# Cutting the last loads of a one-token decode kernel differently: a quarter block by a DMA of 124 rows and one of four

## The chip, the cores and the metric

The kernel runs on one core of one Trainium2 chip. The metric is the device time of one execution in microseconds, as the median of several runs. Lower is better.

## The reference

One token `x` of 1024 elements goes through two branches, and a scalar gate mixes their results (shapes are float32; the cut keeps what is computed).

```python
g = sigmoid((x * gate_w).sum(-1))
# branch A: attention over a cache; 32 query heads, 4 key/value heads, 65536 positions, head size 128
q = x @ wq                                   # 1024 -> 32 heads x 128
scores = einsum("bhqd,bhkd->bhqk", q, k) * 128 ** -0.5     # k, v: (1, 4, 65536, 128), each shared by 8 heads
a = einsum("bhqk,bhkd->bhqd", softmax(scores), v).reshape(1, 1, 4096) @ wo
# branch B: a gated feed-forward layer on the one token, scaled by its router weight
r = x @ w_r
y = (silu(x @ w_gate) * (x @ w_up)) @ w_down # 1024 -> 3584 -> 1024
b = x + y * sigmoid(r)
out = g * a + (1 - g) * b
```

Nearly all bytes are the two caches, 134 MB each; with the projections and the feed-forward weights some 346 MB are read once.

## The kernel before

**Streaming.** Everything large comes from HBM through three buffers of 128 partitions x 16384 floats (`stream`, called `st` in the profile). SyncE (SP) issues all these loads from one queue, in the order of one loop (lines 119 to 133). The first 36 loads (`heads`) are wq, the caches and wo of the four key/value groups, 8 MB each. Then come six tiles of `ffn`, 14336 floats per row: two of w_gate, two of w_up and two of w_down. A load waits on SP until TensorE has marked the buffer's last use (`marked`, line 124).

**Blocks of w_down.** w_down is cut into 28 blocks of 128 rows; a block is 1024 floats in each partition (`D` = 1024). Tile 4 holds blocks 0 to 13, tile 5 blocks 14 to 27. These two tiles come by several DMAs, each with a semaphore of its own (`end0`, `end1`, ...), cut at the columns in `ENDS` (line 34). Before, tile 5 comes by six DMAs: blocks 14 to 19, 20 to 23, 24 and 25, 26, the first 768 columns of block 27, and its last 256. In TensorE's program the helper `tail` (lines 364 to 374) waits for a DMA's semaphore when the first column asked of it is that DMA's first column.

**The last products.** TensorE (PE) takes blocks 0 to 23 in matmuls of 512 columns into the PSUM tile `att`, which already holds the attention's result folded over 128 partitions (the loop that ends with `mark(ins, "early")`). VectorE (DVE) then adds `att` to `att_sb`, which holds the gated attention and the residual (`dve.tensor_add` at line 277): this is the early sum. The last four blocks (24 to 27; `EARLY` = 24) go to two other PSUM tiles, `y` for the first 192 columns of each quarter of the output and `acc` for the last 64 (`PIECES`), by four matmuls of 32 output partitions per tile and block; the profile counts each of them twice, so that a block is 8 on `y` and 8 on `acc`. The early sum is brought into the same tiles by eight products with the small matrix `halves` (line 404). Before, these stand with block 26, each ahead of the product of that block with the same output partitions, and TensorE waits for the early sum (`take("d2p")`, line 399) ahead of block 26.

**The end.** ScalarE (ACT) copies `y`, VectorE copies `acc`, and SP writes the 4 KB result with one DMA of four rows and waits for it (lines 134 to 140).

**Small loads.** ScalarE issues two small loads at the start: `xk` of 128 rows and `x_row` of two rows.

Of the kernel before, what the change touches and what calls it, by code (L numbers as in the profile page):

```python
# [8 lines left out]
P = 128  # L9
D = 1024  # L10
G = 4
# [9 lines left out]
NQ = D // 4  # L21
# [6 lines left out]
PER = UNITS // 2  # L28
BUFS = 3

TAIL = 14336
NTAIL = 3 * KB * F // TAIL

ENDS = {NTAIL - 2: [8 * D, TAIL], NTAIL - 1: [6 * D, 10 * D, 12 * D, 13 * D, 13 * D + 768, TAIL]}

PIECES = [(0, 192), (192, NQ)]

EARLY = 24
# [13 lines left out]
def gated_mix_kernel(nc, x, vecs, heads, ffn, out):  # L52
# [21 lines left out]
    pe, act, dve, pool, sp = nc.tensor, nc.scalar, nc.vector, nc.gpsimd, nc.sync  # L74

    stream = [nc.alloc_sbuf_tensor(f"st{b}", [P, 2 * CH], F32, align_bytes=256)[:, :] for b in range(BUFS)]
# [35 lines left out]
    names = ["done", "fed", "x0", "x1", "x2", "acted", "pooled", "marked", "d2p", "d2a", "d2s", "self"]  # L112
    names += [f"ld{b}" for b in range(BUFS)] + [f"end{i}" for i in range(sum(map(len, ENDS.values())))]
    sems = {n: nc.alloc_semaphore(n) for n in names}
# [4 lines left out]
    ends = []  # L119
    for i in range(G * PER + NTAIL):  # L120
        b = i % BUFS
        if i >= BUFS:
            g, l = divmod(i - BUFS, PER)
            sp.wait_ge(sems["marked"], MARK[f"{LAST[l]} {g}" if g < G else ["gate 0", "gate 1", "up 0"][l]])
        if i < G * PER:
            sp.dma_start(stream[b], heads[i]).then_inc(sems[f"ld{b}"], 16)
        elif i - G * PER not in ENDS:
            sp.dma_start(stream[b][:, :TAIL], ffn[i - G * PER]).then_inc(sems[f"ld{b}"], 16)
        else:
            cuts = ENDS[i - G * PER]  # L130
            for c0, c1 in zip([0] + cuts, cuts):
                sp.dma_start(stream[b][:, c0:c1], ffn[i - G * PER, :, c0:c1]).then_inc(sems[f"end{len(ends)}"], 16)  # L132
                ends.append((i, c0, c1))
    sp.wait_ge(sems["acted"], ACTED["first"])
    sp.wait_ge(sems["d2s"], 1)
# [45 lines left out]
    c0, c1 = PIECES[0]  # L181
# [97 lines left out]
    c0, c1 = PIECES[1]  # L279
# [5 lines left out]
    def mark(ins, name):  # L285
        marks.append(name)
        ins.then_inc(sems["marked"])

    def take(name, n=1):
        pe.wait_ge(sems[name], n).then_inc(sems[name], -n)  # L290
# [73 lines left out]
    def tail(first, n):  # L364
        i, c = divmod(first, TAIL)
        assert c + n <= TAIL
        if i < min(ENDS):
            if c == 0:
                take(f"ld{(G * PER + i) % BUFS}", 16)
        else:  # L370
            for e, (i1, c0, _) in enumerate(ends):
                if (i1 - G * PER, c0) == (i, c):
                    pe.wait_ge(sems[f"end{e}"], 16)
        return stream[(G * PER + i) % BUFS][:, c : c + n]


    for i, part in enumerate(("gate", "up")):
        ps = (ps_f, ps_u)[i]
        for k in range(KB):
            for e in range(2):  # L380
                for j in range(4):
                    ins = pe.matmul(  # L382
                        ps[32 * j : 32 * j + 32, e, :FN], xp[:, k, :], tail((i * KB + k) * F + (2 * j + e) * FN, FN),
                        start=(k == 0), stop=(k == KB - 1),
                    )
            if k % 4 == 3:
                mark(ins, f"{part} {k // 4}")
    take("d2p")
    for b in range(EARLY):
        for f in range(2):  # L390
            j = 2 * (b % 2) + f
            ins = pe.matmul(  # L392
                att[32 * j : 32 * j + 32, :], hp[:, 32 * b : 32 * b + 32], tail(2 * KB * F + b * D + f * 512, 512),
                start=(b < 2), stop=(b >= EARLY - 2),
            )
    mark(ins, "early")
    for b in range(EARLY, FB):
        if b == EARLY + 2:
            take("d2p")
        for bank, (c0, c1) in zip(banks, PIECES):  # L400
            n = c1 - c0
            for j in range(4):
                if b == EARLY + 2:
                    pe.matmul(  # L404
                        bank[32 * j : 32 * j + 32, :n], halves[:, j // 2, :],
                        att_sb[:, j % 2 * NQ + c0 : j % 2 * NQ + c1], start=False, stop=False,
                    )
                at = 4 * c0 + j * n if b == FB - 1 else j * NQ + c0
                ins = pe.matmul(  # L409
                    bank[32 * j : 32 * j + 32, :n], hp[:, 32 * b : 32 * b + 32], tail(2 * KB * F + b * D + at, n),  # L410
                    start=(b == EARLY), stop=(b == FB - 1),
                )
            if b == FB - 1:
                mark(ins, "first" if c0 == 0 else "last")
# [32 lines left out]
```

## Time and profile before

| | us |
|---|---|
| median of 3 runs | 805.84 (805.73 to 806.34) |
| the profiled execution | 805.78 |
| its span, first to last instruction | 804.5 |

| engine | busy us | share of the span |
|---|---|---|
| PE (matmul) | 407.5 | 51% |
| DVE | 72.3 | 9% |
| ACT | 44.8 | 6% |

The span leaves out what lies around the program's instructions: 805.78 - 804.5 = 1.28 us. PE is TensorE's matmul row, PEld its weight loads, SPq an instruction that SP's queue issues (a DMA here). In a timeline row stand the start and the duration in us, the engine, the line, the operation, the tiles written and read, the shape, the count, and in brackets how long the engine sat idle before it and what ended that. In a row of stretches the last three columns are the granted clock of TensorE, the mean busy share of the 16 DMA engines and the rate in GB/s; a packet counts in the stretch in which it starts, so that a share can pass 1.

### The profile page before, as it was taken

Reading aid. Unit: us, or ns where it says so; the run is one execution under the profiler, and the core shown is the slowest. Engines: PE = TensorE matmul, PEld = TensorE weight load, DVE = VectorE, ACT = ScalarE, POOL = GpSimd, SP = SyncE. Lnnn points to the kernel's source line nnn. Section 1 sums busy time; section 2 is a strip of 40 time slices with the busy share of each in tenths; the row PEclk is TensorE's granted clock in tenths of the full one; section 3 lists DMA queues with packets and bytes.
Section 4 is the critical chain, followed back from the end, with each engine's and each line's share of the span. In section 5 each row is a group of like instructions: output and inputs, shape, how many; then the busy total and the mean of one; then the engine's idle time right before and its main releaser. Section 6 shows DMA issues by size and latency. Waiting matters only on the chain. (4 is left out here: it accounts for less than half of the span.)

```text
span 804.5 us, 6124 instructions
## 1 busy us (share of the span) xinstructions
PE 407.5 (51%) x2826; PEld 122.0 (15%) x2826; DVE 72.3 (9%) x135; ACT 44.8 (6%) x100; POOL 2.5 (0%) x13
## 2 busy tenths in 40 slices
PE   0544464455654564545544454456444545464466
PEld 0211111111111121111111111112111111121122
DVE  0200010000000020000100110000000100000310
ACT  0000030000000030000000110000000300000000
POOL 1000000000000000000000000000000000000000
PEclk9977767768767677677877586777776866787778
DMA  9999999999999999999999999999999999999998
GB/s 418 417 418 466 415 424 460 417 428 453 420 430 450 424 431 446 427 430 446 427 430 443 430 430 443 430 431 430 440 433 427 443 430 430 429 448 426 439 413 342
DMA packets 7078, 346.20 MB, mean 430 GB/s; under 512 B 918, under 2 KB 1050, under 8 KB 1308
## 3 DMA queue, kind: packets, MB, share of 16 engines
q1 hardware_dynamic: 6920, 346.04, 99.4%
q8 instruction: 8, 0.13, 0.1%
q10 hardware_dynamic: 148, 0.02, 0.0%
q14 instruction: 2, 0.02, 0.0%
HBM read 346.05 MB, written 0.00 MB: 430 GB/s over the span
## 5 line engine op out<-in xcount | busy, mean ns | idle before, releaser
L326 PE MATMUL ps_u<-st,qp 128*32 128x512 f32 x1024 | 152.5, 759 | 149.1 <-PEq L290 149.1
L338 PE MATMUL acc<-st,pt 128*32 128x512 f32 x1024 | 152.3, 757 | 144.1 <-PEq L290 144.1
L338 PEld LDWEIGHTS acc<-st,pt 128*32 128x32 f32 x1024 | 43.5, 135 | 250.0 <-issue 250.0
L326 PEld LDWEIGHTS ps_u<-st,qp 128*32 128x32 f32 x1024 | 41.4, 135 | 256.3 <-issue 256.3
L171 ACT ACTIVATE s<-ps_u 128x512 f32<-128x512 f32 x32 | 19.1, 597 | 560.4 <-PE ps_u L326 560.4
L240 DVE TENSOR_REDUCE mx<-s 128x1 f32<-128x512 f32 x32 | 22.0, 686 | 284.2 <-ACT s L171 284.2
L255 DVE STREAM_TRANSPOSE pt<-s 128x512 f32<-128x512 f32 x32 | 22.7, 711 | 198.0 <-PE acc L338 194.4
L310 PE MATMUL ps_u<-st,xp 128*32 128x512 f32 x128 | 23.3, 893 | 22.1 <-PEq L290 22.1
L382 PE MATMUL ps_u<-st,xp 128*32 128x448 f32 x128 | 17.1, 703 | 16.9 <-PEq L290 16.9
L382 PE MATMUL ps_f<-st,xp 128*32 128x448 f32 x128 | 16.8, 691 | 13.3 <-PEq L290 13.3
L176 ACT ACTIVATE s<-s,nb 128x512 f32<-128x512 f32 x32 | 22.6, 708 | 10.4 <-DVE nb L250 10.4
L392 PE MATMUL att<-st,s 128*32 128x512 f32 x96 | 14.9, 776 | 7.5 <-DMA st<-in_ffn 4.9
L355 PE MATMUL att<-st,op 128*32 128x512 f32 x128 | 14.6, 594 | 2.4 <-PEq L290 2.4
L301 PE MATMUL ps_m<-dsum,ones 128*128 128x2 f32 x2 | 0.6, 350 | 23.5 <-PEq L290 23.5
L310 PEld LDWEIGHTS ps_u<-st,xp 128*32 128x32 f32 x128 | 5.9, 158 | 40.1 <-issue 40.1
L382 PEld LDWEIGHTS ps_u<-st,xp 128*32 128x32 f32 x128 | 5.3, 139 | 28.6 <-issue 28.6
L259 DVE COPY s<-acc 128x512 f32<-128x512 f32 x4 | 2.8, 692 | 71.6 <-PE acc L338 71.6
L382 PEld LDWEIGHTS ps_f<-st,xp 128*32 128x32 f32 x128 | 5.2, 135 | 25.1 <-issue 25.1
L229 DVE COPY s<-ps_u 128x512 f32<-128x512 f32 x4 | 2.8, 692 | 53.5 <-PE ps_u L310 53.5
L179 ACT ACTIVATE s<-ps_f 128x896 f32<-128x896 f32 x1 | 0.9, 917 | 105.4 <-PE ps_f L382 105.4
L392 PEld LDWEIGHTS att<-st,s 128*32 128x32 f32 x96 | 3.7, 134 | 18.6 <-issue 10.7
L332 PE MATMUL ps_m<-md,ones 128*128 128x128 f32 x8 | 1.8, 311 | 8.2 <-PEq L290 8.2
(69 smaller groups left out, 68.9 us busy)
## 6 DMA issues: line engine op xcount, KB each, us to landing
st<-in_ffn SPq DMA_DIRECT2D x4, 7168.0 KB, 43.3
st<-in_ffn SPq DMA_DIRECT2D x2, 3072.0 KB, 37.1
st<-in_ffn SPq DMA_DIRECT2D x1, 4096.0 KB, 34.9
st<-in_ffn SPq DMA_DIRECT2D x1, 2048.0 KB, 36.9
st<-in_ffn SPq DMA_DIRECT2D x1, 1024.0 KB, 38.9
st<-in_heads SPq DMA_DIRECT2D x36, 48.1
st<-in_ffn SPq DMA_DIRECT2D x1, 512.0 KB, 39.7
st<-in_ffn SPq DMA_DIRECT2D x1, 384.0 KB, 40.2
```

What stands on the lines that cost most here:

```text
L171: tell(act.activation(scores[:, c, :], ps_s[c % 2], AF.Copy), f"s{c} {g}")
L176: act.activation(t, t, AF.Exp, bias=nb, scale=SCALE, accum_out=sums[:, c : c + 1]), f"e{c} {g}"
L229: to_pe(dve.tensor_copy(q_sb, ps_s[0]))
L240: ins = dve.tensor_reduce(mx[:, c : c + 1], scores[:, c, :], AX.X, ALU.max)
L255: to_pe(dve.transpose(pts[:, c % 2, :], scores[:, c, :]))
L259: to_pe(dve.tensor_copy(o_sb, acc.rearrange("p (s d) -> p s d", s=4)))
L310: ins = pe.matmul(ps_s[0][32 * j : 32 * j + 32, :], xp[:, k, :], unit(0)[:, k * D + f * 512 : k * D + (f + 1) * 512], start=(k < 2), stop= ...
L326: ins = pe.matmul(ps_s[c % 2][32 * j : 32 * j + 32, :], qp[:, 32 * s : 32 * s + 32], unit(1 + c)[:, (4 * s + j) * 512 : (4 * s + j + 1) * ...
L338: ins = pe.matmul(acc[32 * j : 32 * j + 32, :], pts[:, c % 2, 32 * m : 32 * m + 32], unit(1 + NCH + c)[:, m * 512 : (m + 1) * 512], start= ...
L355: ins = pe.matmul(att[32 * j : 32 * j + 32, :], op[:, h, :], unit(UNITS - 1)[:, h * D + f * 512 : h * D + (f + 1) * 512], start=False, sto ...
L382: ins = pe.matmul(ps[32 * j : 32 * j + 32, e, :FN], xp[:, k, :], tail((i * KB + k) * F + (2 * j + e) * FN, FN), start=(k == 0), stop=(k == ...
L392: ins = pe.matmul(att[32 * j : 32 * j + 32, :], hp[:, 32 * b : 32 * b + 32], tail(2 * KB * F + b * D + f * 512, 512), start=(b < 2), stop= ...
```

## The change

Tile 5 of the feed-forward weights is cut at other columns, so that it comes by eight DMAs in place of six. Block 24 comes in two parts. Its first 768 columns are one DMA of 128 rows. Its last 256 columns (`NARROW`) are two DMAs on one semaphore: partitions 0 to 123, then partitions 124 to 127 (`ROWS`); TensorE waits for 32 on that semaphore. Blocks 25 and 26 come by one DMA. The two parts of block 27 stay as they were. The eight products of the early sum, and the wait for it, move from block 26 to block 25.

```diff
-ENDS = {NTAIL - 2: [8 * D, TAIL], NTAIL - 1: [6 * D, 10 * D, 12 * D, 13 * D, 13 * D + 768, TAIL]}
+ENDS = {NTAIL - 2: [8 * D, TAIL], NTAIL - 1: [6 * D, 10 * D, 11 * D - NQ, 11 * D, 13 * D, 13 * D + 768, TAIL]}
+
+NARROW, ROWS = (NTAIL - 1, 11 * D - NQ), [(0, 124), (124, P)]
...
             for c0, c1 in zip([0] + cuts, cuts):
-                sp.dma_start(stream[b][:, c0:c1], ffn[i - G * PER, :, c0:c1]).then_inc(sems[f"end{len(ends)}"], 16)
+                for r0, r1 in ROWS if (i - G * PER, c0) == NARROW else [(0, P)]:
+                    sp.dma_start(
+                        stream[b][r0:r1, c0:c1], ffn[i - G * PER, r0:r1, c0:c1]
+                    ).then_inc(sems[f"end{len(ends)}"], 16)
                 ends.append((i, c0, c1))
...
                 if (i1 - G * PER, c0) == (i, c):
-                    pe.wait_ge(sems[f"end{e}"], 16)
+                    pe.wait_ge(sems[f"end{e}"], 16 * len(ROWS) if (i, c) == NARROW else 16)
...
     for b in range(EARLY, FB):
-        if b == EARLY + 2:
+        if b == EARLY + 1:
             take("d2p")
         for bank, (c0, c1) in zip(banks, PIECES):
             n = c1 - c0
             for j in range(4):
-                if b == EARLY + 2:
+                if b == EARLY + 1:
                     pe.matmul(
                         bank[32 * j : 32 * j + 32, :n], halves[:, j // 2, :],
                         att_sb[:, j % 2 * NQ + c0 : j % 2 * NQ + c1], start=False, stop=False,
                     )
```

## The prediction

> **What bounds the kernel now.** I read the page first, its queues and its chain of waits.
>
> ```profile
> span 804.5 us, 6124 instructions
> DMA  9999999999999999999999999999999999999998
> q1 hardware_dynamic: 6920, 346.04, 99.4%
> q8 instruction: 8, 0.13, 0.1%
> q10 hardware_dynamic: 148, 0.02, 0.0%
> ```
>
> The DMA engines are busy in all 40 slices, and only the last slice falls under nine tenths. The change leaves the bytes as they are, so all that it can move lies in the last few microseconds. The chain of waits, asked for its last stretch, and the timeline of that stretch show what they hold.
>
> ```profile
> 759.67 0.33 SPq L132
> ...
> 760.52 38.89 DMA st<-in_ffn
> ...
> 801.73 0.11 PE acc L409 x6
> 801.84 0.37 PE y L409 x8
> ```
>
> ```profile
> 792.17 6.77 PE L392 MATMUL att<-st,s 128*32 128x512 f32 x40 [4.46 <-DMA st<-in_ffn]
> 797.02 0.16 PEld L392 LDWEIGHTS att<-st,s 128*32 128x32 f32 x8 [1.23 <-DMA st<-in_ffn]
> ...
> 799.01 0.69 DVE L277 TENSOR_TENSOR s<-att,s 128x512 f32<-128x512 f32 x1 [20.00 <-PE att L392]
> 799.45 0.16 PEld L409 LDWEIGHTS y<-st,s 128*32 128x32 f32 x8 [1.42 <-DMA st<-in_ffn]
> 799.46 0.53 PE L409 MATMUL y<-st,s 128*32 128x192 f32 x8 [0.51 <-DMA st<-in_ffn]
> ...
> 799.92 0.51 PE L409 MATMUL y<-st,s 128*32 128x192 f32 x8
> ...
> 800.35 0.49 PE L404 MATMUL y<-s,halves 128*32 128x192 f32 x2
> 800.72 0.11 PEld L409 LDWEIGHTS y<-st,s 128*32 128x32 f32 x1 [0.26 <-DMA st<-in_ffn]
> ...
> 801.67 0.53 PE L409 MATMUL y<-st,s 128*32 128x192 f32 x8
> ...
> 802.02 0.29 PE L409 MATMUL acc<-st,s 128*32 128x64 f32 x8
> 802.27 0.33 ACT L182 ACTIVATE s<-y 128x192 f32<-128x192 f32 x1 [58.66 <-PE y L409]
> ```
>
> TensorE waits for loads at 797.02 (blocks 20 to 23), at 799.45 (24 and 25) and at 800.72 (26). From there it has no gap: the eight early-sum products and block 26 fill 800.72 to 801.67, and block 27 follows at once, by the chain behind TensorE's own work (801.73, 801.84). The loads end at the same moment, as the stretches of the end show (the last three columns are TensorE's clock, the DMA share and GB/s):
>
> ```profile
> 799.90:800.10 0.20, 0.20 (x20) 0.17 (x15) 0.00 (x0) 0.00 (x0) 0.00 (x0) 1.00 0.82 312
> 800.10:800.30 0.20, 0.20 (x13) 0.17 (x9) 0.00 (x0) 0.00 (x0) 0.00 (x0) 1.00 0.66 256
> 800.30:800.50 0.20, 0.20 (x13) 0.17 (x6) 0.00 (x0) 0.00 (x0) 0.00 (x0) 1.00 0.57 225
> ...
> 800.70:800.90 0.20, 0.20 (x5) 0.17 (x8) 0.00 (x0) 0.00 (x0) 0.00 (x0) 1.00 0.52 210
> 800.90:801.10 0.20, 0.20 (x11) 0.17 (x7) 0.00 (x0) 0.00 (x0) 0.00 (x0) 1.00 0.39 154
> 801.10:801.30 0.20, 0.20 (x15) 0.20 (x7) 0.00 (x0) 0.00 (x0) 0.00 (x0) 1.00 0.45 159
> ...
> 801.60:801.80 0.20, 0.20 (x17) 0.20 (x13) 0.00 (x0) 0.00 (x0) 0.00 (x0) 1.00 0.00 0
> ```
>
> The sixteen DMA engines don't end together. Times 16, the shares say that six or seven are done by about 800.3, two or three more (the middle ones) by about 800.9, and six or seven, the late ones, run to about 801.6. So there are early engines 1.2 to 1.6 us ahead of the last, middle ones some 0.7 to 1.2 ahead, and late ones. Every load is complete only when the last engine has delivered. TensorE's clock is at full grant there.
>
> **How many engines the new loads use.** The queues' packets tell how a load is spread. q1 carries 48 loads of 128 rows (36 of heads, four whole tiles, two and six parts) and the four-row result: 48 x (128 + 16) + 4 + 4 = 6920. q10 carries 128 rows and two rows: 128 + 16 + 2 + 2 = 148. So beside its rows a load leaves 16 small packets for 128 rows, four for four rows and two for two, one per engine at work, and each engine gets the same number of rows. A number of at most 16 that divides 124 into equal shares is 1, 2 or 4; the trace has no such load, and the ends are one engine and, with unequal shares, sixteen. I take four, since the two-row and four-row loads took the largest number that divides them. The Trainium skill, "DMA: Bandwidth & Descriptors", section "Why a DMA increments its semaphore by 16 and not by 1", states that rule, the largest number up to 16 that divides both sides' outer size, and that from SP it is the lowest-numbered engines; the packet counts agree with the first half, and no view here numbers engines.
>
> Then 128 rows of 1 KB fall on four engines, 32 each, where block 24's part of a whole load put eight on each of sixteen.
>
> **Part 1, the loads.** Per engine the stretches between TensorE's wake-ups give the prices: 799.45 - 797.02 = 2.43 us for 64 KB (eight rows of 8 KB), 800.72 - 799.45 = 1.27 for 32 KB, 801.67 - 800.72 = 0.95 for 24 KB (rows of 3 KB), and at most 802.02 - 801.67 = 0.35 for eight rows of 1 KB, since TensorE was at work there too. A row of 1 KB thus costs between 2430 / 64 = 38 and 350 / 8 = 44 ns, and 32 of them 1.2 to 1.4; I take 1.3.
>
> On the twelve other engines, the late ones among them, what follows 797.02 is now 0.95 (block 24's first part), 2.43 (25 and 26), 0.95, 0.35: 0.32 us less than before. Blocks 25 and 26 are there at 797.02 + 0.95 + 2.43 = 800.40. On the four it is 1.3 more, less what they are ahead:
> - early engine (1.4 ahead): 800.30, before the others, so it costs nothing
> - middle engine (0.95 ahead): 797.02 - 0.95 + 0.95 + 1.3 + 2.43 = 800.75
> - late engine: 801.70
>
> The issue costs nothing:
>
> ```profile
> L132 SPq DMA_DIRECT2D st<-in_ffn x8: 328/432/858, 742.7 to 761.9; - x8
> DMA to landing us min/median/max: 32.5/39.3/41.8
> ```
>
> Two more issues are two times 0.43 us on SP, and block 27's loads go out 0.9 us later; what hides it are the 32.5 us or more that a load stands in the queue. Without that cover the end would move by those 0.9. Behind them on SP stands only the wait for the result.
>
> **Part 2, TensorE.** A block without the early sum takes 799.92 - 799.46 = 0.46 us, the one with it 0.95 from its data (its first pair of products with `halves`, at 800.35, ran ahead of the wait). Before, 24 and 25 were done while 26 was under way, and 0.95 followed the last load but two. Now blocks 25 and 26 arrive together, so 0.95 + 0.46 = 1.41 us follow their landing, ahead of block 27. With 0.32 us saved on the load and 0.46 added behind it, block 27 starts at 800.40 + 1.41 = 801.81 even where the four engines delay nothing: 0.14 later than 801.67. With a middle engine among the four it starts at 800.75 + 1.41 = 802.16, 0.49 later; with a late one at 801.70 + 1.41 = 803.11, 1.44 later. Block 27's own loads are no bound in these cases: on the middle engine they land at 801.70 and 802.05, and their products start at 802.16 and 802.51. From there on the end is as before.
>
> The wait for the early sum now stands one block earlier, with all of TensorE's remaining work behind it. TensorE ends block 23 at 792.17 + 6.77 = 798.94, does block 24 until about 799.4, and waits until VectorE is done at 799.01 + 0.69 = 799.70. That is 0.7 us before 800.40, so block 25's load hides it; without that cover it would cost 0.3. The narrow load is wanted in block 24, at about 799.1, and on a middle engine it lands at 797.02 - 0.95 + 0.95 + 1.3 = 798.3.
>
> **Sum.** The forecast is the middle engine: +0.49. The profiled execution took 805.78, its span plus 1.28, and the median is 805.84, 0.06 more and inside the runs' spread; 805.84 + 0.49 = 806.3. About 0.2%, or 1.6 us, is what a measurement of this kernel can tell from no change, so this would count as none.
>
> **The rivals.**
>
> *A late engine among the four*: block 27 starts 1.2 to 1.44 later (the late ones lie within 0.2), 807.0 to 807.3. For it: six or seven of sixteen are late, so four drawn blindly would nearly always hold one. Against it: q8 has eight loads of some 16 KB, and following packets through the trace by end and start (no view groups them by engine), the seven late engines are those that carried one each, while the two engines of the two-row load are one early and one middle. If small loads always take the same first engines, and q8 goes from one engine to its neighbour, the other two of the four are clear of it in most places that its run can have.
>
> *Only early engines in the four, or packets and PE overlap better*: +0.14 down to a gain of 0.32, if TensorE's 1.41 could shrink to the 0.95 between block 26's load and the next: 805.5 to 806.0. Against it, the rows from 800.72 to 801.67 have no gap to take out, and one of the two known engines is middle.
>
> *Not confined*: the 124 rows go to sixteen engines, eight each. Then every engine has 0.35 more than without the narrow load, and blocks 25 and 26 land at 800.40 + 0.35 = 800.75: also 806.3, by another way.
>
> *A fixed hold, slower*: each of the two small loads keeps its engine for the round trip of a load that stands alone, instead of streaming with its neighbours. The nearest row is SP's wait for the 4 KB result:
>
> ```profile
> SPq L140 <- DMA out<-s: 1.1, 1, 1.1
> ```
>
> Two holds of 1.1 on the middle engine give 800.75 + 2.2 = 802.95 and block 27 at 804.36: +2.7, 808.5. It decides the sign from a hold of (1.6 - 0.49) / 2 = 0.56 each. Against it: block 27's two loads followed each other within 0.35. The same page of the skill, section "Anatomy of one DMA", gives a fixed cost of about 2 us per DMA; by that the two would cost up to 4 us on these engines, and the trace's back-to-back small loads contradict it inside a full queue. Fewer than four engines (two of 62 and two rows: 64 x 0.041 = 2.6 in place of 1.3) would end near there too, at +1.8, 807.6.
>
> **Chances.** Middle engine 0.47, not confined 0.06, only early engines or a small gain 0.12, a late engine 0.17: all of these lie within 0.2%, 0.82 together, of which I give 0.03 to a late engine with packets dearer than 44 ns, over 1.6 us, so 0.79 remain. Fixed hold or fewer engines 0.14, which with those 0.03 makes slower 0.17. Faster by over 1.6 us 0.04: nothing in the rows gives it, since the engines' whole unevenness is 1.6. The range leaves out most of the gains and the fixed hold: from 805.6, a little under the early case, to 807.4, a late engine with dear packets. The likeliest case alone is 806.0 to 806.7 (prices and lead at their ends).
>
> **What would show it.** Right: TensorE's first wait after block 24 ends near 800.8, the products of the early sum and of both blocks follow without a gap, block 27 starts near 802.2 behind TensorE and not behind a load, and the DMA share falls to nothing earlier than before on most engines. Wrong: the wait for 25 and 26 ends near 800.4 (early engines) or past 801.4 (a late one), block 24 waits at its last quarter, or block 27 waits for its load.

## The result, and the profile after

| | us |
|---|---|
| before, median of 22 runs | 805.84 (805.63 to 806.34) |
| changed, median of 22 runs | 806.98 (806.57 to 807.89) |
| ratio | 1.0014, 95% interval 1.0008 to 1.0019 |
| the profiled execution of the changed kernel | 807.16, span 805.9 |

The changed kernel is slower by 1.14 us, or 0.14%. The forecast was 806.3 with a range of 805.6 to 807.4. The interval of the ratio keeps off 1, so the direction is clear, but the amount lies under the 0.2% that the prediction took as its bound.

The page of the changed kernel, its span, its DMA row and its main queue:

```profile
span 805.9 us, 6126 instructions
DMA  9999999999999999999999999999999999999997
q1 hardware_dynamic: 7056, 346.04, 99.4%
```

The packets settle how the 124 rows were spread. Beside 48 loads of 128 rows, 48 x (128 + 16) = 6912, there are 124 + 4 rows, the four-row result with its four small packets, and 8 packets left: 6912 + 128 + 8 + 8 = 7056. So both new loads ran on four engines each, as the Trainium skill's rule ("DMA: Bandwidth & Descriptors", section "Why a DMA increments its semaphore by 16 and not by 1") has it.

The timeline of the end, changed kernel:

```profile
797.52 0.16 PEld L397 LDWEIGHTS att<-st,s 128*32 128x32 f32 x8 [1.63 <-DMA st<-in_ffn]
...
799.51 0.69 DVE L282 TENSOR_TENSOR s<-att,s 128x512 f32<-128x512 f32 x1 [20.59 <-PE att L397]
799.58 0.11 PEld L414 LDWEIGHTS y<-st,s 128*32 128x32 f32 x1 [0.19 <-DMA st<-in_ffn]
...
800.35 0.48 PE L409 MATMUL y<-s,halves 128*32 128x192 f32 x2
801.73 0.11 PEld L414 LDWEIGHTS y<-st,s 128*32 128x32 f32 x1 [1.28 <-DMA st<-in_ffn]
...
802.64 0.49 PE L414 MATMUL y<-st,s 128*32 128x192 f32 x5
...
803.08 0.37 PE L414 MATMUL y<-st,s 128*32 128x192 f32 x4
...
803.76 0.22 DVE L285 COPY s<-acc 128x64 f32<-128x64 f32 x1 [3.56 <-PE acc L414]
```

Blocks 20 to 23 are there at 797.52, blocks 25 and 26 at 801.73. Block 25 with the early sum takes until 802.64, block 26 until 803.08, where block 27 starts. From the landing of blocks 20 to 23 to the start of block 27 it is 803.08 - 797.52 = 5.56 us, where before had 801.67 - 797.02 = 4.65. That is 0.91 us of the loss. The other 0.50 us of this execution was there at 797.52 already. The last packet of blocks 20 to 23 ended 0.34 us later here than before (796.99 and 796.65), and single executions of one kernel differ by that much: in two profiles of the uncut version below it ended at 797.08 and at 796.60. The other 0.16 us is that TensorE woke later after that packet, 0.53 us in place of 0.37. The DMA rate in the stretch from 797 to 799, before and then changed (the last two columns are the share of the engines' time and GB/s):

```profile
797.00:799.00 2.00, 1.94 (x20) 0.42 (x16) 0.00 (x0) 0.00 (x0) 0.00 (x0) 1.00 0.97 402
```

```profile
797.00:799.00 2.00, 1.48 (x16) 0.54 (x19) 0.00 (x0) 0.00 (x0) 0.00 (x0) 1.00 1.07 364
```

A busy engine moved less: 402 / 0.97 = 414 GB/s per full share before, 364 / 1.07 = 340 after. The packet records say why. Before, each of the 128 packets of 8 KB near the end took 309 ns. In the changed kernel 77 of the 128 took longer, up to 427 ns. These are the packets of blocks 25 and 26, on engines whose own bytes had become fewer or more, and no step of the prediction had them grow.

The packets also tell which engine came last. No view groups them by engine, but within a full queue each packet of an engine starts as the one before it ends, so that they can be followed. Of the four engines with the narrow loads (the two DMAs of block 24's last columns), two were early and two were middle ones. These two middle engines ended their last packet of blocks 25 and 26 at 801.11 and 801.25, every other engine by 800.75. So the wait that ends at 801.73 is for a middle engine with the narrow loads.

### The profile page after: what moved, and what is told of

The parts are those of the page before. It is cut to its first block, busy times and chain, and to the rows that moved or that the text cites. A ratio compares the mean times of both kernels' runs of the same rounds, so it can differ in the third digit from the quotient of the medians.

```text
span 805.9 us, 6126 instructions
## 1 busy us (share of the span) xinstructions
PE 396.1 (49%) x2826; PEld 119.3 (15%) x2826; DVE 72.4 (9%) x135; ACT 44.8 (6%) x100; POOL 2.5 (0%) x13
## 2 busy tenths in 40 slices
DMA packets 7214, 346.20 MB, mean 430 GB/s; under 512 B 926, under 2 KB 1186, under 8 KB 1444
## 5 line engine op out<-in xcount | busy, mean ns | idle before, releaser
L331 PE MATMUL ps_u<-st,qp 128*32 128x512 f32 x1024 | 148.2, 740 | 155.1 <-PEq L295 155.1
L343 PE MATMUL acc<-st,pt 128*32 128x512 f32 x1024 | 147.1, 735 | 149.6 <-PEq L295 149.6
L343 PEld LDWEIGHTS acc<-st,pt 128*32 128x32 f32 x1024 | 41.0, 132 | 252.6 <-issue 252.6
L315 PE MATMUL ps_u<-st,xp 128*32 128x512 f32 x128 | 21.5, 830 | 20.0 <-PEq L295 20.0
L397 PEld LDWEIGHTS att<-st,s 128*32 128x32 f32 x96 | 3.7, 132 | 19.2 <-issue 10.4
L360 PEld LDWEIGHTS att<-st,op 128*32 128x32 f32 x128 | 4.7, 117 | 10.6 <-issue 10.6
## 6 DMA issues: line engine op xcount, KB each, us to landing
st<-in_ffn SPq DMA_DIRECT2D x1, 128.0 KB, 25.4
```

Of the source, the lines that this page charges most:

```text
L315: ins = pe.matmul(ps_s[0][32 * j : 32 * j + 32, :], xp[:, k, :], unit(0)[:, k * D + f * 512 : k * D + (f + 1) * 512], start=(k < 2), stop= ...
L331: ins = pe.matmul(ps_s[c % 2][32 * j : 32 * j + 32, :], qp[:, 32 * s : 32 * s + 32], unit(1 + c)[:, (4 * s + j) * 512 : (4 * s + j + 1) * ...
L343: ins = pe.matmul(acc[32 * j : 32 * j + 32, :], pts[:, c % 2, 32 * m : 32 * m + 32], unit(1 + NCH + c)[:, m * 512 : (m + 1) * 512], start= ...
L360: ins = pe.matmul(att[32 * j : 32 * j + 32, :], op[:, h, :], unit(UNITS - 1)[:, h * D + f * 512 : h * D + (f + 1) * 512], start=False, sto ...
L397: ins = pe.matmul(att[32 * j : 32 * j + 32, :], hp[:, 32 * b : 32 * b + 32], tail(2 * KB * F + b * D + f * 512, 512), start=(b < 2), stop= ...
```

## Experiments

The theory was that engines which write into partitions that another engine is filling slow it (collision). Its rivals were that the order of the cuts or the place of the early sum cost it all, that each of the four engines only pays for its own bytes, and that the reading side is in the way. Times are medians; the kernels of one set shared a chip and its runs of the kernel before.

| set | kernel | us | before, same set | difference | ratio, 95% interval |
|---|---|---|---|---|---|
| a | one load of 128 rows instead of 124 and 4 | 806.44 | 805.96 | +0.48 | 0.9997 to 1.0015 |
| a | changed, early sum at block 26 | 806.92 | 805.96 | +0.96 | 1.0003 to 1.0021 |
| a | before, early sum at block 25 | 805.79 | 805.96 | -0.17 | 0.999 to 1.0008 |
| a | before + loads into partitions 0 to 3 | 808.29 | 805.96 | +2.33 | 1.0017 to 1.0041 |
| b | before + loads into 0, 4, 8, 12 | 805.92 | 805.97 | -0.05 | 0.999 to 1.0009 |
| b | before + loads into 64, 68, 72, 76 | 807.53 | 805.97 | +1.56 | 1.001 to 1.0029 |
| c | one load of 128 rows, again | 806.25 | 805.93 | +0.32 | 0.9996 to 1.0014 |
| c | cut at partition 64 | 806.69 | 805.93 | +0.76 | 1.0001 to 1.0019 |
| c | cut at partition 112 | 806.83 | 805.93 | +0.90 | 1.0002 to 1.002 |
| c | changed, again | 806.96 | 805.93 | +1.03 | 1.0004 to 1.0022 |

**The cuts without the split.**

```diff
-NARROW, ROWS = (NTAIL - 1, 11 * D - NQ), [(0, 124), (124, P)]
+NARROW, ROWS = (NTAIL - 1, 11 * D - NQ), [(0, P)]
```

> The changed kernel, but the last 256 columns of block 24 come by one load of 128 rows on sixteen engines. Theory A, packets in each other's way: the narrow split slows the other engines' packets, so with it gone the DMA rate keeps to its share (434 GB/s at a share of 1.04 in the kernel before, 334 at 1.05 in the changed one between 797.5 and 798.0), and what stays is the order of the cuts: 0.95 + 0.35 + 2.43 + 1.41 = 5.14 us from the landing of blocks 20 to 23 to the start of block 27, where before had 4.65: +0.5, about 806.3. Theory B, the cuts and the early sum's place cost it all, and the split is free: about 807.0, as the changed kernel.

The timeline of its end, and the stretch from 797 to 799:

```profile
797.43 0.16 PEld L397 LDWEIGHTS att<-st,s 128*32 128x32 f32 x8 [1.53 <-DMA st<-in_ffn]
...
801.20 0.11 PEld L414 LDWEIGHTS y<-st,s 128*32 128x32 f32 x1 [0.83 <-DMA st<-in_ffn]
...
802.11 0.37 PE L414 MATMUL y<-st,s 128*32 128x192 f32 x4
...
802.54 0.37 PE L414 MATMUL y<-st,s 128*32 128x192 f32 x4
```

```profile
797.00:799.00 2.00, 1.65 (x20) 0.55 (x20) 0.00 (x0) 0.00 (x0) 0.00 (x0) 1.00 1.07 441
```

Block 27 starts 802.54 - 797.43 = 5.11 us after the landing of blocks 20 to 23; 5.14 was expected. The rate is 441 / 1.07 = 412 GB/s per full share, as before, and no packet of 8 KB is longer than 309 ns. So the cuts cost 0.3 to 0.5 us; the interval of each uncut run alone includes 1, but the two sets and the timeline agree. The split costs the rest, 0.5 to 0.7 (806.92 - 806.44 in set a, with the early sum at block 26, and 806.96 - 806.25 in set c).

**The place of the early sum.** Both edits are the one number below, once in the changed kernel (back to block 26) and once in the kernel before (on to block 25).

```diff
-        if b == EARLY + 1:
+        if b == EARLY + 2:
```

> The changed kernel with the early sum put back to block 26. Theory A (the products behind one landing of two blocks count, wherever the early sum stands): still 0.95 + 0.46 = 1.41 us or up to 0.1 more after the landing of blocks 25 and 26, so 807.0 to 807.1. Rival C, the move of the early sum costs something of its own (the wait for VectorE, at 799.5 to 800.2 in the changed kernel): 0.3 or more faster than the changed kernel, 806.7 or less.

> The kernel before with only the early sum moved to block 25; cuts and loads as before. Theory A: TensorE does block 24, then block 25 with the early sum, until about 800.9, and block 26 until 801.3, so block 27 starts behind its load at 801.67 as before: 805.8, within 0.1. Rival C, the earlier wait costs: 806.1 or more. A gain is possible only as far as the load of block 27 lands ahead of 801.67.

Put back, it gains nothing that can be told: 0.96 us over the kernel before, beside the changed kernel's 1.03 and 1.14, where rival C asked for a gain of 0.3 or more. Moved alone, it costs nothing. The timeline of the kernel before with the move shows where its time went:

```profile
796.85 0.39 PEld L392 LDWEIGHTS att<-st,s 128*32 128x32 f32 x8 [1.19 <-DMA st<-in_ffn]
...
799.93 0.56 PE L404 MATMUL y<-s,halves 128*32 128x192 f32 x8
...
801.12 0.36 PE L409 MATMUL acc<-st,s 128*32 128x64 f32 x8
801.55 0.16 PEld L409 LDWEIGHTS y<-st,s 128*32 128x32 f32 x8 [0.23 <-DMA st<-in_ffn]
```

TensorE is through with block 26 just before block 27's load comes, and waits for it: 801.55 - 796.85 = 4.70, as before's 4.65. What the early sum left, the load took. So the early sum's place is not what the cuts cost; what is left is that both blocks come by one load.

**Where the bytes are written.** Three loads of four rows of 8 KB are added to the kernel before, from the same weights each time and used for nothing. They put 24 KB more on each of four engines, just what the change does (32 KB less the 8 KB of before). Only the partitions differ.

```diff
             for c0, c1 in zip([0] + cuts, cuts):
+                if (i - G * PER, c0) == (NTAIL - 1, 10 * D):
+                    for t in range(BUFS):
+                        sp.dma_start(
+                            stream[t][0:4, TAIL:], ffn[NTAIL - 1, 0:4, 0 : 2 * CH - TAIL]
+                        ).then_inc(sems["extra"], 16)
```

The other two have `0:16:4` and `64:80:4` in place of `0:4`. SP waits for the new semaphore ahead of the result. SP's queue has 6944 packets in each of the three, 3 x (4 + 4) more than before, so each additional load ran on four engines.

> The kernel before with three loads more ahead of that of blocks 24 and 25: four rows of 8 KB each, from the same rows of the weights into partitions 0 to 3 of the unused ends of the three buffers. They are used for nothing. So four engines get 24 KB each more, and all of it goes to partitions that one engine serves in the loads of 128 rows. Theory A, what collides is the writing side, engines that write to the same group of partitions: 96 KB at the 64 KB per 2.43 us of one engine is 3.6 us into one group, so blocks 24 and 25 are there 2.2 to 3.3 us later than 799.45 (the lead of that engine taken off), 808.0 to 809.1. Rival D, each engine only pays for its own bytes: 24 KB are 0.91 us on engines with a lead of 0.7 or more, so at most +0.2, 805.8 to 806.0. By the Trainium skill, "SBUF — State Buffer", section "Door 1: The DMA port swizzle", partitions 0 to 3 lie behind one of 16 ports.

> As the run into partitions 0 to 3, with the same sources and sizes, but into partitions 0, 4, 8 and 12, so that the four engines write into four different groups of partitions, each the one that this engine serves in a load of 128 rows if the engines are taken in order. Theory A (the writing side collides): no packets of others are slowed; each of the four pays 24 KB, 0.91 us, against its lead: +0.0 to +0.2, 805.8 to 806.0. Rival D2, the four engines' reading of the weights is what gets in the others' way: packets of other engines grow here as well, and the time is the same as with partitions 64 to 76. By the Trainium skill, "SBUF — State Buffer", section "Door 1: The DMA port swizzle", these four partitions lie behind four ports.

> The same three loads into partitions 64, 68, 72 and 76: four groups of partitions that other engines serve in the loads of 128 rows. Theory A (the writing side collides): these groups get 24 KB more each, so four other engines' packets are slowed by up to 0.91 us in all, and the four that carry the loads take up to twice 0.91; the 1.8 us exceed a middle engine's lead of 0.7 to 1.2 by 0.6 or more: blocks 24 and 25 land 0.4 to 1.1 us later, 806.2 to 806.9. Rival D2 (the reading side) or D (only own bytes): the same time as with partitions 0, 4, 8 and 12.

The landing of blocks 20 to 23 and of blocks 24 and 25, and the stretch from 797 to 799. Into partitions 0, 4, 8 and 12:

```profile
796.89 0.23 PEld L398 LDWEIGHTS att<-st,s 128*32 128x32 f32 x8 [1.22 <-DMA st<-in_ffn]
799.50 0.16 PEld L415 LDWEIGHTS y<-st,s 128*32 128x32 f32 x8 [1.53 <-DMA st<-in_ffn]
```

```profile
797.00:799.00 2.00, 1.88 (x20) 0.36 (x14) 0.04 (x1) 0.00 (x0) 0.00 (x0) 1.00 0.99 414
```

Into 64, 68, 72 and 76:

```profile
798.23 0.16 PEld L398 LDWEIGHTS att<-st,s 128*32 128x32 f32 x8 [2.39 <-DMA st<-in_ffn]
800.65 0.16 PEld L415 LDWEIGHTS y<-st,s 128*32 128x32 f32 x8 [1.41 <-DMA st<-in_ffn]
```

```profile
797.00:799.00 2.00, 0.77 (x8) 0.29 (x12) 0.00 (x0) 0.00 (x0) 0.00 (x0) 1.00 0.96 363
```

Into 0 to 3:

```profile
798.23 0.16 PEld L398 LDWEIGHTS att<-st,s 128*32 128x32 f32 x8 [2.46 <-DMA st<-in_ffn]
802.03 0.16 PEld L415 LDWEIGHTS y<-st,s 128*32 128x32 f32 x8 [2.78 <-DMA st<-in_ffn]
```

```profile
797.00:799.00 2.00, 0.94 (x12) 0.29 (x12) 0.00 (x0) 0.00 (x0) 0.00 (x0) 1.00 0.87 227
```

The same bytes from the same place cost nothing into four groups of partitions (418 GB/s per full share), 1.56 us into four others (378) and 2.33 us into one (261). Packets of 8 KB took 309 ns in the first, up to 629 in the second and up to 1186 in the third. (The profiled execution of the second, 806.89 us, is the fastest of its ten runs, which reach 808.62.) That rules out the reading side, and also that the four engines' own bytes are what costs in the second and third. In the first they all but hide in the lead, as the prediction had it: blocks 24 and 25 land 2.61 us after blocks 20 to 23, where before had 2.43, and the time is the same. The second cost more than was expected, because it also delayed the load ahead of it: blocks 20 to 23 land at 798.23 instead of some 797, since early engines start their next load while late ones still finish this one. By the Trainium skill, "SBUF — State Buffer", section "Door 1: The DMA port swizzle", the partitions lie behind 16 ports in groups of eight, 0 to 3 behind one, and 0, 4, 8, 12 and 64, 68, 72, 76 behind four each. The three times agree; that the first set is the four engines' own is what its unchanged packets say, and no view numbers engines.

**Equal bytes, other partitions.** To see the collision in the change's own split without an uneven load, the cut was moved to partitions where both loads run on sixteen engines (7080 packets, 16 more than in the uncut version).

```diff
-NARROW, ROWS = (NTAIL - 1, 11 * D - NQ), [(0, 124), (124, P)]
+NARROW, ROWS = (NTAIL - 1, 11 * D - NQ), [(0, 64), (64, P)]
```

and `[(0, 112), (112, P)]`; the uncut version and the changed kernel ran beside them.

> The changed kernel with the 256 columns cut at partition 64 instead of 124: two loads of 64 rows, on sixteen engines by the counting rule, four rows to each. Every engine has the same bytes as with one load of 128 rows, but engine e now writes partitions 4e to 4e+3 of each half, so that in each load half of the engines write into groups that others serve. Theory A (the writing side collides): packets of 8 KB grow beyond 309 ns, and the time is 0.1 to 0.3 over the uncut version. Rival E (what cost 0.5 to 0.6 in the changed kernel is that four engines carry it all): as the uncut version, no packet longer than before.

> The changed kernel with the cut at partition 112: loads of 112 and 16 rows, both on sixteen engines by the counting rule, seven neighbouring partitions and one to each. Equal bytes on each engine again, but nearly every engine writes into groups of other engines. Theory A: 8 KB packets grow beyond 309 ns, time 0.1 to 0.4 over the uncut version. Rival E: as the uncut version.

> The uncut version (128 rows in one load) once more, beside the others on the same chip: 806.3 to 806.5, and no packet longer than before.

> The changed kernel once more, beside the others on the same chip: 0.4 to 0.7 over the uncut version, with 8 KB packets of 309 to some 430 ns. If it lies within 0.2 of the uncut version, the difference between the first two calls was one between chips and the collision costs less than taken.

Stretches from 797 to 799: cut at 64, cut at 112, uncut, changed.

```profile
797.00:799.00 2.00, 1.43 (x16) 0.54 (x19) 0.00 (x0) 0.00 (x0) 0.00 (x0) 1.00 1.04 377
```

```profile
797.00:799.00 2.00, 2.00 (x20) 0.54 (x19) 0.00 (x0) 0.00 (x0) 0.00 (x0) 0.95 1.07 390
```

```profile
797.00:799.00 2.00, 2.00 (x24) 0.66 (x24) 0.00 (x0) 0.00 (x0) 0.00 (x0) 0.95 0.99 411
```

```profile
797.00:799.00 2.00, 1.79 (x20) 0.59 (x24) 0.00 (x0) 0.00 (x0) 0.00 (x0) 1.00 1.05 375
```

Per full share: 363, 364, 415 and 357 GB/s. The uncut version has no longer packet; the others have them up to 413, 486 and 426 ns. Against the uncut version, the cut at 64 costs 0.44 us, the one at 112 costs 0.58, and the changed kernel 0.71. So the collision costs something without any uneven load, and in both equal versions more than was expected. That an engine writes a run of neighbouring partitions in such loads was assumed; no view shows it, and the longer packets fit it. The Trainium skill's advice against two transfers to disjoint halves of the partitions ("DMA: Bandwidth & Descriptors", section "Rules for kernel authors") fits the 0.44 us of the cut at 64.

How much of the changed kernel's loss is collision can't be had by taking these prices off it, since another engine comes last there. The packets show it, counted from the end of the last packet of blocks 20 to 23:

| us to | uncut (two traces) | cut at 64 | cut at 112 | changed, changed again, early sum at 26 |
|---|---|---|---|---|
| the last packet of blocks 25 and 26 | 3.74, 3.74 | 3.97 | 3.97 | 4.26, 4.04, 4.23 |
| TensorE's start on block 25 | 4.12, 4.12 | 4.48 | 4.48 | 4.74, 4.52, 4.71 |
| the engine that came last | late | late | late | middle, with the narrow loads |

With equal bytes the late engines are slowed by 0.23 us, and TensorE starts a further 0.13 later after the last packet. In the split into 124 and 4 rows the late engines have fewer bytes, which makes up for their longer packets, and a middle engine is last by 0.26 to 0.50 us. An estimate of what it would have taken without longer packets, from its lead in each trace (0.74, 0.91, 0.75), the 1.37 us that the narrow loads took on the early engines, and the uncut prices 0.95 and 2.45, gives 4.03, 3.86 and 4.02. So of the 0.40 to 0.62 us over the uncut version, 0.1 to 0.3 are that engine's greater share, some 0.2 are longer packets, and 0.1 is the later start, which came with the longer packets in every trace and whose reason is not shown. In the run into 0, 4, 8 and 12 the 24 KB more took 0.93 us on a middle engine with a lead of 0.80; blocks 24 and 25 landed 0.18 us later for it, ahead of TensorE's wait for block 26, and that cost nothing.

None of this points to a version that beats the kernel before. The earlier early sum alone is 0.17 us ahead, which its interval doesn't tell from nothing.

## Why the prediction was right or wrong

**Where the loss was placed.** The last microseconds, behind the landing of blocks 20 to 23: right. The bytes are the same, and before that point the two kernels are alike.

**TensorE's part.** Predicted, 1.41 us from the landing of blocks 25 and 26 to block 27; measured 803.08 - 801.73 = 1.35 in the changed kernel and 802.54 - 801.20 = 1.34 in the uncut one. TensorE is the bound there and block 27 waits for no load, as foretold. With the loads as priced, this gives the +0.5 of the uncut version, which ran at +0.48 and +0.32.

**The load's prices.** 0.95, 0.35 and 2.43 us sum to 3.73 from one landing to the other; the uncut version had 801.20 - 797.43 = 3.77. The rows priced them well as long as nothing collided.

**The four engines.** Four was right, by the packet counts. Two early and two middle engines carried the narrow loads, and a middle one delivered last in all three traces of this split. This is the case that was taken as likeliest. By the prediction's own sign, a wait that ends past 801.4, it would have been read as a late engine; the packets say that it was not. Another sign of being wrong did show, a wait at block 24's last quarter (0.19 us at 799.58), but it stood under the wait for block 25 and cost nothing.

**The step that failed** is that a load's price on an engine is its own bytes at the prices of before, and with it the size of the middle engine's term, "797.02 - 0.95 + 0.95 + 1.3 + 2.43 = 800.75". That is 3.73 us after the landing of blocks 20 to 23; measured were 801.73 - 797.52 = 4.21 between TensorE's waits (4.26 between the packets), so it came 0.48 too late on the path that was forecast. In the profile after, the last of the middle engines was 0.74 us ahead of the late ones and not 0.95, inside the bounds that were named. The narrow loads took it 1.53 us and not 1.3: 0.07 more even on the early engines, whose packets did not grow, and 0.16 from longer packets. Its eight rows of 8 KB took 2.52 and not 2.43, 0.07 of that from longer packets.

The same step failed on the other engines: "On the twelve other engines, the late ones among them, what follows 797.02 is now 0.95 ..., 2.43 ..., 0.95, 0.35: 0.32 us less than before." The late ones had fewer bytes but longer packets, and took 3.76 us from blocks 20 to 23 to blocks 25 and 26 where 0.95 + 2.43 = 3.38 were priced. That was not the bound here, since they were still 0.50 us ahead of the middle engine; in the two equal cuts it was. The rival "not confined" is out by the packet counts. The fixed hold did not show: on the early engines the second narrow load started as the first ended, and the three additional loads into 0, 4, 8 and 12 cost nothing. (The section of the Trainium skill that the prediction names there gives its 2 us for DMAs that GpSimd issues; these are SP's.)

**The issue.** Two issues of 0.43 us were foretold. The changed kernel's own row:

```profile
L135 SPq DMA_DIRECT2D st<-in_ffn x10: 328/432/13709, 742.6 to 777.5; - x10
DMA to landing us min/median/max: 25.4/34.1/42.2
```

One issue took 13.7 us, and the last went out at 777.5 instead of 761.9. The cover that was named, the time that a load stands in the queue, was still 25.4 us at the least, so the price of nothing stood, but the size was wrong by far. Long issues are not what makes packets collide: the additional loads that collided cost 1.56 and 2.33 us with all issues done by 764.5.

**The early sum.** Its wait was hidden, by more than said: VectorE was done at 799.51 + 0.69 = 800.20, and the load came at 801.73.

**The sum.** Predicted +0.49. Measured +1.14: the cuts 0.3 to 0.5, the split 0.5 to 0.7. That the measured time lies inside the range is luck: the range reached up that far for a late engine's price, a mechanism that did not occur.

## What to carry to other kernels

A DMA engine that runs ahead of the others is not free capacity. In these runs extra bytes on such engines cost nothing as long as they went into partitions that those engines fill in a full load, and up to 2.33 us when they went where other engines were writing. Keep a split by partitions such that every engine keeps to the partitions that it has in a full load, or leave the load whole. Price the engines one by one: the fullest of those that get more must still finish within its own lead. And when two loads are joined so that the last products start together, count all the work behind the joint landing, since it stood under the next load before.

## What the runs showed that was not expected

Packets of 8 KB that took 309 ns took up to 430 in the changed kernel, up to 630 when the additional bytes went into four groups of partitions that other engines filled, and up to 1190 when all went into one group, while the same bytes into other groups left them at 309. And with the narrow load split, SP's later issues stalled: one of them took 13.7 us in the changed kernel, 11.1 with the cut at 64 and 10.4 with the cut at 112, where no issue of the uncut version took more than 0.63. It is neither the number of loads alone nor the four engines' greater share, since three additional loads did not stall and the two equal cuts did. The cause was not looked for.
